# Two attention/SwiGLU layers in fp32: the second projection's chunk 2 is turned earlier, its load moves on the DMA queue, and one closing step changes form

## The chip, the core and the metric

The kernel runs on one core of one Trainium2 chip. The metric is the device time of one launch in microseconds (us). Before the change the median of three runs is 1949.36 us (1948.67 to 1949.93).

## The reference

Two identical layers on `x` of shape 1 x 2048 x 448, in fp32; the weights of the second layer are those of the first:

```python
def A(x, wq, wk, wv, wo):          # 16 heads of 28, one shared key and value head
    q = (x @ wq).reshape(B, S, 16, 28).transpose(0, 2, 1, 3)
    k, v = x @ wk, x @ wv
    p = softmax(einsum("bhqd,bkd->bhqk", q, k) * 28 ** -0.5)
    return einsum("bhqk,bkd->bhqd", p, v).transpose(0, 2, 1, 3).reshape(B, S, 448) @ wo
def B(x, w_gate, w_up, w_down):    # inner width 1792
    return (silu(x @ w_gate) * (x @ w_up)) @ w_down
x = x + A(layernorm(x)); x = x + B(layernorm(x))
x = x + A(layernorm(x)); x = x + B(layernorm(x))
```

## The kernel before

The 2048 rows are four chunks of 512 (`NC`), each of four tiles of 128 rows. `xres` holds the running `x` in SBUF. Every fp32 product is made of three passes over split operands: a high part (`xh`, `wh`) and a remainder (`xl`, `wl`).

The order of instructions on each engine is the order in which the Python code issues them (`manual_schedule`): nothing is reordered, and the engines wait for each other by semaphores alone. So the order is written out by hand, with three helpers. `self.soon` is a list of `[count, function]`: each `unit` lowers all counts by one and runs, in list order, those that fall below zero. `a.plan[n, 0]` and `a.plan[n, 1]` hold functions that `project` runs ahead of and behind its n-th tile. `self.pend` holds the down step of the unit before and the additions that follow it.

Each layer runs in three stages: the projection (16 tiles numbered by `self.seen`, 0 to 15, four for each chunk), the scores with softmax and P-V, and the feed-forward. The feed-forward goes through 14 column tiles `fc` of the inner width in seven groups of two, and in each group through the four chunks; one `unit` makes one `fc` of one chunk, and `down` multiplies its result by `w_down` into four PSUM banks `d[0..3]`, one for each tile of 128 rows. `down` works in two half steps. In each, pairs of matmuls lie side by side, one over rows 0 to 63 of the contraction and one over rows 64 to 127 (`side_by_side`, L332). Behind the first half step ScalarE reads one column of each bank (`between`, L339), and the second half waits for that. For the very last step of the second layer alone, `by_tile` (L888) makes 12 matmuls over all 128 rows instead, bank after bank.

The change lies where the first layer's feed-forward passes into the second layer's projection. There `hand_over(c)` is called for each chunk when its last group is done:

- `turn` makes the normalized chunk (`xn`, VectorE L230), transposes it in 32 x 32 blocks (L268, into a buffer named `xh`), and sends it to DRAM with four DMAs of SyncE's queue (`send`, L274, to `xt`).
- `load` fetches it back with the transpose completed, into two idle query buffers `qstack` (SyncE L954, L955, L957).
- `parts` splits that into `xh` on ScalarE (L292, L296) and `xl` on VectorE (L293, L302).

Chunk 3 is turned on TensorE instead (`ready`, L230, then transposes L248 ahead of tile 8). Its additions (`accumulate`) come behind the closing down step: banks 0 and 1 are added by VectorE (L901), banks 2 and 3 are copied by ScalarE to a `stage` buffer (L904) and added by GpSimd (L905).

Each projected tile is stored (`q`, L545 to L556): ScalarE copies it twice (L545, L546), SyncE stores it to `qd` (L547) and, for the tiles with keys, to `kt` (L550); for the tiles with values VectorE transposes a strip (L553, `vt`) and GpSimd copies it in four pieces (L556, `vsb`). After tile 2 the queue also fetches eight keys, `few` (L405), from which VectorE builds `kdiag` (L409), used by the `maxima` matmuls (L438) behind tile 6.

Of the kernel before, what the change touches and what calls it, by code (L numbers as in the profile page):

```python
# [23 lines left out]
NC = S // 512  # L24
NG = H // 4
NF = F // P
# [29 lines left out]
def forward(  # L56
# [31 lines left out]
    phase, banks, threes, live, turn = ExitStack(), [], [], set(), {}  # L88
# [114 lines left out]
    def xtile(pool, again=None):  # L203

        return (
            pool.tile([P, 4, 512], F32R, name="xh"),
            pool.tile([P, 3, 512], F32R, name="xl"),
            again,
        )

    def norm_steps(c, pool=pers, twice=True):

        got = {}
        cs = slice(4 * c, 4 * c + 4)

        def stat(t):
            nc.vector.bn_stats(stats[:, 4 * c + t, :], xres[:, 4 * c + t, :])
            nc.vector.bn_aggr(mv[:, 4 * c + t, :], stats[:, 4 * c + t, :])

        def scale():  # L220
            rstd = pers.tile([P, 4], F32, name="rstd", bufs=2)
            nc.gpsimd.tensor_scalar(rstd, mv[:, cs, 1], 1.0, EPS, ALU.mult, ALU.add)
            nc.gpsimd.tensor_tensor(rstd, rstd, halfn, ALU.pow)
            got["r"] = rstd

        def apply(t):
            if t == 0:
                got["x"] = pool.tile([P, 4, 512], F32, name="xn")
            o, i, r = got["x"][:, t, 0:D], xres[:, 4 * c + t, :], got["r"][:, t : t + 1]
            nc.vector.tensor_scalar(o, i, mv[:, 4 * c + t, 0:1], r, ALU.subtract, ALU.mult)  # L230
            if twice:
                nc.gpsimd.tensor_copy(got["x"][:, t, D:512], o[:, 384:D])

        fs = [lambda t=t: stat(t) for t in range(4)] + [scale]
        return fs + [lambda t=t: apply(t) for t in range(4)], got
# [30 lines left out]
    def turn_tile(got, tb, t):  # L266

        nc.vector.transpose(tb[:, :, 32 * t : 32 * t + 32], got["x"][:, t, 0:D].rearrange("p (b w) -> p b w", w=32))  # L268

    def send(tb, raw):  # L270

        to = raw.rearrange("(b d) (g n) -> g d b n", d=32, g=4)
        for g in range(4):
            nc.sync.dma_start(to[g], tb[32 * g : 32 * g + 32])  # L274
# [11 lines left out]
    def halved(tiles, r, ks, copy, sub):  # L286

        xh, xl, xd = tiles
        for k in ks:
            raw = r[k] if isinstance(r, list) else r[:, k, :]  # L290
            if k < 3:
                copy(xh[:, k, :], raw)  # L292
                sub(xl[:, k, :], raw, xh[:, k, :], ALU.subtract)  # L293
                continue
            if xd is None:
                copy(xh[:, 3, :], raw)  # L296
                high = xh[64:128, 3, :]
            else:
                copy(xd[64:128, :], raw[64:128, :])
                copy(xh[0:64, 3, :], raw[0:64, :])  # L300
                high = xd[64:128, :]
            sub(xh[64:128, 3, :], raw[64:128, :], high, ALU.subtract)  # L302
# [24 lines left out]
    def side_by_side(lower, upper):  # L327

        assert len(lower) == len(upper)
        for two in zip(lower, upper):  # L330
            for po, (a, b), start, stop in two:
                nc.tensor.matmul(po, a, b, start=start, stop=stop, skip_group_check=True)  # L332
# [3 lines left out]
    def between(*pos):  # L336

        for i, po in enumerate(pos):
            nc.scalar.copy(seen[:, i : i + 1], po[:, 0:1])  # L339
# [504 lines left out]
    groups = [range(f, min(f + FG, NF)) for f in range(0, NF, FG)]  # L844

    class FeedForward:
# [6 lines left out]
        def down(self, fs, fc, d, hh, hl):  # L853


            _, _, dh, dl = self.W[fc]
            if self.layer == 1 and d is self.dn.get(NC - 1) and fs is groups[-1]:
                return [lambda: self.by_tile(fs, fc, d, ((hh, dh), (hh, dl), (hl, dh))), lambda: None]
            self.flip = 1 - self.flip
            one, two = ((0, 1), (2, 3)) if self.flip else ((2, 3), (0, 1))  # L860

            def step(ts, first):
                lists = []
                for upper, half in enumerate(ts):
                    rs = slice(64 * upper, 64 * upper + 64)
                    lists.append(
                        [
                            (
                                d[t][:, 0:D],
                                (a[rs, P * t : P * t + P], b[rs, :]),  # L870
                                first and fc == fs[0] and z == 0,
                                not first and fc == fs[-1] and z == 2,
                            )
                            for t in half
                            for z, (a, b) in enumerate(((hh, dh), (hh, dl), (hl, dh)))
                        ]
                    )
                side_by_side(*lists)
                if first:
                    between(*d)  # L880

            return [lambda: step((one, two), True), lambda: step((two, one), False)]
# [36 lines left out]
        def hand_over(self, c):  # L919

            a = self.nxt
            fs, got = norm_steps(c, twice=c == NC - 1)
            for f in fs[:5]:
                f()
            a.pool = self.stage

            if c == NC - 1:

                def ready():
                    for f in fs[5:]:  # L930
                        f()
                    a.norms[c] = got

                a.X[c] = xtile(self.xbp)
                a.plan[5, 1] = [ready]
                return
            to = dram.tile([D, 512], F32, name=f"xt1_{c}")
            raw = [q.bitcast(F32)[:, z, :] for q in qts[1:] for z in range(2)]

            def turn():  # L940
                for f in fs[5:]:
                    f()
                pool = (xpool, self.x1p, self.xbp)
                tb = pool[min(c + 1, 2)].tile([P, 4, 512], F32R, name="xh").bitcast(F32)
                tb = tb.rearrange("p a (b n) -> p (a b) n", n=P)[:, 0 : D // 32, :]
                for t in range(4):
                    turn_tile(got, tb, t)
                send(tb, to)
                a.X[c] = xtile(pool[c])
                if c < 2:  # L950
                    load()

            def load():
                nc.sync.dma_start(qts[1].bitcast(F32), to[0:256, :].rearrange("(k p) n -> p k n", p=P))  # L954
                nc.sync.dma_start(raw[2], to[256:384, :])  # L955
                for half in (slice(0, 64), slice(64, 128)):
                    nc.sync.dma_start(raw[3][half, :], to[384:448, :])  # L957

            def parts():
                halved(a.X[c], raw, range(4), nc.scalar.copy, nc.vector.tensor_tensor)  # L960

            self.soon.append([1, turn])
            if c == 2:
                a.plan[4, 1] = [load]
                a.plan[7, 0] = [parts]
                return
            self.soon.append([3, parts])
            self.soon.append([4 - c, lambda: [a.project() for _ in range(2 - c)]])
# [160 lines left out]
    fs, got = norm_steps(0)  # L1129
# [23 lines left out]
    for c in range(1, NC):  # L1153
        fs, got = norm_steps(c)
# [39 lines left out]
```

## Time and profile before

| what | value |
|---|---|
| runs | 1949.36 us median, 1948.67 to 1949.93 |
| the profiled execution | 1949.26 us, its span 1947.5 us |
| TensorE busy | 1934.0 us, 99% of the span |
| ScalarE, VectorE, GpSimd busy | 1251.9, 980.8, 560.1 us |
| granted TensorE clock | 0.999 |
| first tile of the second projection | 969.1 us from the span's start |
| closing down step of the first layer | 987.1 to 990.6 us |
| first score matmul of the second layer | 1026.9 us |

The timeline gives for each instruction its start, its duration, its engine and line, and in square brackets how long the engine sat idle before it and what released it. Rows of equal neighbours are merged with a count, and the duration is then that of the whole row. Matmuls overlap in the pipeline, so the distance between two starts is what one costs. A row "SPq" is the issue of a DMA by SyncE; the transfer comes after it.

### The profile page before, as it was taken

The page shows a single profiled execution, that of the slowest core. Times are in us where ns is not written, and L with a number is a line of the kernel's source. Part 1 is how long each engine was busy: PE and PEld are TensorE (multiplying, and loading weights), DVE is VectorE, ACT ScalarE, POOL GpSimd, SP SyncE. Part 2 cuts the span into 40 slices and gives each one's busy share as a digit, 9 for nine tenths or more (in the row PEclk, how much of TensorE's full clock was granted, in tenths as well). Part 3 has the DMA queues.
Part 4 walks back from the last instruction along what each step waited for, and adds up shares of the span by engine and source line. Part 5 has one row for each costly group of instructions (what it writes and reads, how often), then busy time and mean ns, then how long its engine had stood idle before and what let it go on. Part 6 is the DMA issues. An engine that isn't in the chain of part 4 may idle for free. (4 is left out here: it accounts for less than half of the span.)

```text
span 1947.5 us, 43868 instructions
## 1 busy us (share of the span) xinstructions
PE 1934.0 (99%) x18393; PEld 1311.6 (67%) x18393; DVE 980.8 (50%) x1675; ACT 1251.9 (64%) x1871; POOL 560.1 (29%) x596
## 2 busy tenths in 40 slices
PE   9999999999999999999999999999999999999998
PEld 7544545445468999999974445454454688888887
DVE  6665575665754222322666555757657432232223
ACT  4899898998953333333359998989989333333332
POOL 4213123122215333433341221122231352333420
PEclk9999999999999999999999999999999999999999
DMA  5111011021122011100251110110221220011102
GB/s 166 57 35 30 22 40 41 23 58 31 32 81 73 17 32 32 33 22 22 63 157 43 34 34 21 40 39 24 57 50 31 77 62 25 17 32 32 33 1 77
DMA packets 105475, 87.54 MB, mean 45 GB/s; under 512 B 25304, under 2 KB 85464, under 8 KB 105272
## 3 DMA queue, kind: packets, MB, share of 16 engines
q1 hardware_dynamic: 103576, 83.25, 15.5%
q8 instruction: 145, 2.38, 0.5%
q10 hardware_dynamic: 1696, 1.43, 0.2%
q14 instruction: 58, 0.48, 0.1%
HBM read 59.48 MB, written 23.33 MB: 43 GB/s over the span
## 5 line engine op out<-in xcount | busy, mean ns | idle before, releaser
L662 ACT ACTIVATE pt<-three 128x1536 f32<-128x1536 f32 x512 | 731.2, 1515 | 52.7 <-PE three L640 52.7
L695 PE MATMUL bank<-pt,vsb 128*32 128x512 f32 x3072 | 490.8, 598 | 0.0
L695 PE MATMUL bank<-pair,vsb 128*32 128x512 f32 x1024 | 487.4, 598 | 0.6 <-ACT pair L663 0.6
L640 PE MATMUL bank<-qstack,keys 32*128 32x512 f32 x1536 | 471.8, 425 | 0.0
L640 PE MATMUL three<-qstack,keys 32*128 32x512 f32 x4608 | 428.7, 408 | 0.5 <-ACT stage L546 0.3
L640 PEld LDWEIGHTS bank<-qstack,keys 32*128 32x128 f32 x1536 | 243.3, 183 | 248.1 <-issue 124.6
L661 DVE COPY pair<-bank 128x512 f32<-128x512 f32 x512 | 354.3, 692 | 95.1 <-PE bank L640 60.0
L332 PE MATMUL bank<-xh,wgh 64*128 64x512 f32 x1712 | 357.4, 389 | 0.0
L1025 DVE TENSOR_TENSOR sg<-bank,sg 128x512 f32<-128x512 f32 x112 | 77.4, 691 | 485.4 <-ACT sg L1024 474.7
L332 PE MATMUL bank<-xh,wgl 64*128 64x512 f32 x1391 | 310.7, 390 | 0.0
L332 PE MATMUL bank<-wdh,h 64*128 64x448 f32 x1760 | 303.3, 363 | 1.0 <-DVE h L1031 0.6
L663 ACT ACTIVATE pair<-pair 128x1024 f32<-128x1024 f32 x256 | 289.6, 1131 | 0.0
L640 PEld LDWEIGHTS three<-qstack,keys 32*128 32x128 f32 x4608 | 261.8, 183 | 14.2 <-DVE xres L611 1.5
L332 PE MATMUL bank<-xl,wgh 64*128 64x512 f32 x1284 | 268.5, 389 | 0.0
L695 PEld LDWEIGHTS bank<-pt,vsb 128*32 128x32 f32 x3072 | 101.7, 109 | 246.2 <-issue 153.2
L905 POOL TENSOR_TENSOR xres<-stage,xres 128x448 f32<-128x448 f32 x107 | 126.7, 1204 | 480.5 <-ACT stage L904 480.2
L703 DVE TENSOR_TENSOR o<-bank,o 128x512 f32<-128x512 f32 x224 | 155.0, 692 | 202.3 <-PE bank L695 202.3
L339 ACT COPY seen<-bank 128x1 f32<-128x1 f32 x654 | 74.9, 164 | 253.3 <-PE bank L332 252.7
L1024 ACT ACTIVATE sg<-bank 128x512 f32<-128x512 f32 x112 | 67.2, 600 | 215.9 <-PE bank L332 210.8
L332 PEld LDWEIGHTS bank<-xh,wgh 64*128 64x128 f32 x1712 | 182.0, 184 | 18.4 <-issue 1.0
L332 PEld LDWEIGHTS bank<-wdh,h 64*128 64x128 f32 x1760 | 183.2, 184 | 15.5 <-issue 1.7
L332 PE MATMUL bank<-wdl,h 64*128 64x448 f32 x880 | 174.7, 367 | 0.0
(149 smaller groups left out, 2105.8 us busy)
## 6 DMA issues: line engine op xcount, KB each, us to landing
o<-rd SPq DMA_DIRECT2D x32, 256.0 KB
qraw<-qd SPq DMA_DIRECT2D x128, 56.0 KB
xt<-tb SPq DMA_DIRECT2D x32, 224.0 KB
wdr<-in_B_w_down_dram SPq DMA_DIRECT2D x28, 224.0 KB
xn<-xt SPq DMA_DIRECT2D x8, 768.0 KB
wr<-in_B_w_gate_dram SPq DMA_DIRECT2D x28, 192.0 KB
wr<-in_B_w_up_dram SPq DMA_DIRECT2D x28, 192.0 KB
qd<-stage SPq DMA_DIRECT2D x20, 224.0 KB
```

The source lines that it names most:

```text
L332: nc.tensor.matmul(po, a, b, start=start, stop=stop, skip_group_check=True)
L339: nc.scalar.copy(seen[:, i : i + 1], po[:, 0:1])
L640: nc.tensor.matmul(three[:, j, :] if j < 3 else one, k[js, kp, ks], q[js, part, :], start=(z == 0), stop=(z == 2), tile_position=(32 * j, 0),)
L661: copies.append(nc.vector.tensor_copy(pt1, one))
L662: es.append(nc.scalar.activation(pt, threes[y], AF.Exp, scale=SCALE))
L663: es.append(nc.scalar.activation(pair, pair, AF.Exp, scale=SCALE))
L695: nc.tensor.matmul(to[32 * j : 32 * j + 32, :], vsb[:, n % NT, :], pts[n][j], start=(y == 0), stop=(y == 1), skip_group_check=True,)
L703: f = nc.vector.tensor_tensor(accs[i][:, 0, :], to, accs[i][:, 0, :], ALU.add)
L905: nc.gpsimd.tensor_tensor(r, s, r, ALU.add)
L1024: nc.scalar.activation(in_order(sg, True), natural(pg[0], True), AF.Silu)
L1025: nc.vector.tensor_tensor(in_order(sg, True), natural(pg[1], True), in_order(sg, True), ALU.mult)
```

## The change

It makes three edits, all at the hand-over from the first layer's feed-forward to the second layer's projection.

```diff
@@ down
-            if self.layer == 1 and d is self.dn.get(NC - 1) and fs is groups[-1]:
+            if d is self.dn.get(NC - 1) and fs is groups[-1] and (self.layer == 1 or fc == NF - 1):
                 return [lambda: self.by_tile(fs, fc, d, ((hh, dh), (hh, dl), (hl, dh))), lambda: None]
@@ hand_over
-            self.soon.append([1, turn])
+            self.soon.insert(0 if c == 2 else len(self.soon), [1, turn])
             if c == 2:
-                a.plan[4, 1] = [load]
+                a.plan[4, 0] = [load]
                 a.plan[7, 0] = [parts]
                 return
```

First, on VectorE, behind the last `h` of the first layer's feed-forward (L1031): chunk 2's `turn` (L230, L268) and chunk 1's split (`xl`, `xh` from `qstack`) change places. `vt` is the value strip of tiles 2 and 3, `few` and `kdiag` belong to the maxima.

```order
 L1025 TENSOR_TENSOR sg<-bank_6453,sg 128x512
 L1031 TENSOR_TENSOR h_11444<-sg,h_11444 128x512
+L230 TENSOR_SCALAR xn<-xres,mv,rstd 128x448 x4
+L268 STREAM_TRANSPOSE xh<-xn 128x14x32 x4
 L293 TENSOR_TENSOR xl<-qstack_101,xh 128x512 x2
 L293 TENSOR_TENSOR xl<-qstack_102,xh 128x512
 L302 TENSOR_TENSOR xh<-qstack_102,xh 64x512
 L553 STREAM_TRANSPOSE vt<-bank_6454 32x512
-L230 TENSOR_SCALAR xn<-xres,mv,rstd 128x448 x4
-L268 STREAM_TRANSPOSE xh<-xn 128x14x32 x4
 L553 STREAM_TRANSPOSE vt<-bank_6451 32x512
 L409 TENSOR_TENSOR kdiag<-few,mask 112x512
```

The eight instructions of the turn move ahead of the split and of the first `vt`; from the second `vt` on the order is the old one.

Second, on SyncE's queue at the same place: the four sends of chunk 2 (L274) and the stores of tile 2, tile 3 (both `qd_0`) and tile 4 (`qd_1`, `kt_1`).

```order
+L274 DMA xt_2_11349<-xh 32x14x128 x4
 L547 DMA qd_0_11361<-stage 112x512
 L405 DMA few<-kt_0_789 112x1x8
-L274 DMA xt_2_11349<-xh 32x14x128 x4
 L547 DMA qd_0_11361<-stage 112x512
-L547 DMA qd_1_11593<-raw 112x512
-L550 DMA kt_1_790<-raw 12x512
 L954 DMA qstack_101<-xt_2_11349 128x2x512
 L955 DMA qstack_102<-xt_2_11349 128x512
 L957 DMA qstack_102<-xt_2_11349 64x512 x2
+L547 DMA qd_1_11581<-raw 112x512
+L550 DMA kt_1_790<-raw 12x512
```

The sends now stand ahead of tile 2's store and of `few`, and the load stands ahead of the two stores of tile 4.

Third, on TensorE, the closing down step of chunk 3 in the first layer: 24 matmuls over half the rows become 12 over all rows. The end of the old rows and the beginning of the new ones, with the four banks of `d`:

```order
-L332 MATMUL bank_78<-wdh,h_11444 128x448
-L332 MATMUL bank_6456<-wdh,h_11444 128x448
-L332 MATMUL bank_79<-wdh,h_11444 128x448
-L332 MATMUL bank_6456<-wdl,h_11444 128x448
-L332 MATMUL bank_79<-wdl,h_11444 128x448
-L332 MATMUL bank_6456<-wdh,h_11444 128x448
-L332 MATMUL bank_79<-wdh,h_11444 128x448
+L888 MATMUL bank_6455<-wdh,h_11444 128x448
+L888 MATMUL bank_6455<-wdl,h_11444 128x448
+L888 MATMUL bank_6455<-wdh,h_11444 128x448
+L888 MATMUL bank_6456<-wdh,h_11444 128x448
+L888 MATMUL bank_6456<-wdl,h_11444 128x448
```

The new rows fill bank after bank; on ScalarE the four one-column reads of `between` (L339) that stood inside this step are gone, so that the copies to `stage` (L904) follow the copies of tile 3 directly.

## The prediction

> **What bounds the kernel now.** I read the page first, then TensorE's waits, then the timeline of each engine between 960 and 1030 us.
>
> ```profile
> span 1947.5 us, 43868 instructions
> PE 1934.0 (99%) x18393; PEld 1311.6 (67%) x18393; DVE 980.8 (50%) x1675; ACT 1251.9 (64%) x1871; POOL 560.1 (29%) x596
> ```
>
> TensorE is the bound, with 13.5 us of its span idle. An edit of order can win only at TensorE's pauses and at steps that TensorE itself does slowly. Around the change there are two such places. The first is the closing down step of the first layer; the last two rows are the second layer's closing steps, already in full rows.
>
> ```profile
> 986.77 0.39 PE L312 MATMUL bank<-xh,wl 128*128 128x512 f32 x1
> 987.09 0.47 PE L332 MATMUL bank<-wdh,h 64*128 64x448 f32 x2
> ...
> 989.21 0.47 PE L332 MATMUL bank<-wdh,h 64*128 64x448 f32 x1 [0.36 <-ACT seen L339]
> ...
> 990.63 0.50 PE L312 MATMUL bank<-xh,wh 128*128 128x512 f32 x1
> ...
> 1936.92 0.37 PE L888 MATMUL bank<-wdh,h 128*128 128x448 f32 x1
> ...
> 1941.64 0.37 PE L888 MATMUL bank<-wdh,h 128*128 128x448 f32 x1
> ```
>
> The step lasts from 987.09 to 990.63, 3.54 us, with a wait for ScalarE's `seen` in its middle. The second place is the start of tile 8, the first tile of chunk 2:
>
> ```profile
> 1001.74 1.91 PE L248 MATMUL bank<-ident,xn 128*128 128x128 f32 x16
> 1004.13 0.50 PE L312 MATMUL bank<-xh,wh 128*128 128x512 f32 x1 [0.47 <-ACT xh L292]
> 1004.85 0.50 PE L312 MATMUL bank<-xl,wh 128*128 128x512 f32 x1 [0.22 <-DVE xl L293]
> ```
>
> The transposes of chunk 3 pass (L248); then tile 8 waits 0.47 us for `xh` of chunk 2 and 0.22 us for its `xl`. From 1004.85 to the score stage at 1026.87 us TensorE runs without a pause of that size, so whatever the second matmul of tile 8 gains or loses, the end gains or loses. That one start, **1004.85 us, is my measuring point**.
>
> **The closing step.** 24 matmuls L888 take 23 gaps from 1936.92 to 1941.64, 0.205 us each; 12 take 2.46 us. The pause at a change between the two forms goes too (986.77 to 987.09 is 0.32 us; between neighbours of one form it is 0.23), so the step starts at 987.0 and tile 4 at 989.46 instead of 990.63. That is 1.17 us won on TensorE, if tile 8 lets it through. Tiles 4 to 7 do: their inputs, the split of chunk 1, come from the row of VectorE, next. The four `seen` copies on ScalarE cost nothing beside that wait.
>
> **The turn ahead of the split, on VectorE.**
>
> ```profile
> 983.36 1.89 DVE L293 TENSOR_TENSOR xl<-qstack,xh 128x512 fp32r<-128x512 f32 x3
> ...
> 986.00 0.72 DVE L553 STREAM_TRANSPOSE vt<-bank 32x512 f32<-32x512 f32 x1
> 986.76 1.85 DVE L230 TENSOR_SCALAR xn<-xres,mv,rstd 128x448 f32<-128x448 f32 x4
> 988.53 2.21 DVE L268 STREAM_TRANSPOSE xh<-xn 128x448 f32<-128x448 f32 x4
> 990.77 0.72 DVE L553 STREAM_TRANSPOSE vt<-bank 32x512 f32<-32x512 f32 x1
> 991.53 0.69 DVE L409 TENSOR_TENSOR kdiag<-few,mask 112x512 fp32r<-112x512 f32 x1
> 992.25 1.16 DVE L901 TENSOR_TENSOR xres<-bank,xres 128x448 f32<-128x448 f32 x2
> ...
> 996.20 0.63 DVE L217 BATCH_NORM_STATS2 stats<-xres 128x6 f32<-128x448 f32 x1 [0.58 <-POOL xres L905]
> ...
> 998.46 1.78 DVE L230 TENSOR_SCALAR xn<-xres,mv,rstd 128x448 f32<-128x448 f32 x4 [1.42 <-POOL rstd L223]
> ...
> 1002.53 0.72 DVE L553 STREAM_TRANSPOSE vt<-bank 32x512 f32<-32x512 f32 x1
> 1004.11 1.94 DVE L293 TENSOR_TENSOR xl<-qstack,xh 128x512 fp32r<-128x512 f32 x3 [0.85 <-ACT xh L292]
> ```
>
> The turn takes 986.76 to 990.74, 3.98 us, and the split 983.36 to 986.00, 2.64 us. In the new order the turn ends at 983.36 + 3.98 = 987.34 instead of 990.74, 3.4 us earlier; the split runs from there to 989.98 and the first `vt` to 990.73, 4.0 us later. The second `vt` still stands at 990.76. The split stays covered: its first third is there at 988.0, and tile 4 reads it from 989.7 on at a third each 0.68 us, against 0.65 us for VectorE. Cover of some 1.6 us is left.
>
> **The load.** Sent 3.4 us earlier and no longer behind tile 4's stores, the load can be issued when the sends have landed.
>
> ```profile
> 969.97 3.01 SPq L274 DMA_DIRECT2D xt<-xh  x4
> 976.19 0.38 SPq L954 DMA_DIRECT2D qstack<-xt  x1
> ...
> 985.80 0.30 SPq L547 DMA_DIRECT2D qd<-stage  x1
> 986.21 0.69 SPq L405 DMA_DIRECT2D few<-kt  x1
> 990.77 3.01 SPq L274 DMA_DIRECT2D xt<-xh  x4
> 993.88 1.13 SPq L547 DMA_DIRECT2D qd<-stage  x1
> ...
> 998.34 0.39 SPq L954 DMA_DIRECT2D qstack<-xt  x1
> ```
>
> For chunk 1 the load followed the first send by 6.22 us. So it goes out at 987.34 + 6.22 = 993.6 instead of 998.34, and with 5.1 us to the first `xh` (998.34 to 1003.46 in ScalarE's row below) the data is there at 998.7. ScalarE's wait is gone, and the 0.47 us with it. But what is late next? VectorE reaches `xl` only when its own row lets it: in the old trace it was free for `xl` at 1003.25, behind the `vt` of 1002.53, and waited just 0.85 us. So the load alone could win at most 0.85 us, and only if VectorE's row up to there is not later. It is later, and this is the part that decides.
>
> **What the sends are moved past.** Tile 2's store and `few` now stand behind the four sends on SyncE's queue. Who waits for them?
>
> ```profile
> 990.16 0.53 ACT L904 COPY stage<-bank 128x448 f32<-128x448 f32 x1 [0.95 <-ACT seen L339]
> 994.37 0.53 ACT L904 COPY stage<-bank 128x448 f32<-128x448 f32 x1 [3.67 <-POOL xres L905]
> ...
> 1003.46 1.70 ACT L292 CAST xh<-qstack 128x512 fp32r<-128x512 f32 x3 [3.42 <-DMA qstack<-xt]
> ```
>
> ```profile
> 986.86 1.43 POOL L556 COPY vsb<-vt 32x64 f32<-32x64 f32 x4 [10.10 <-DVE vt L553]
> 991.56 1.53 POOL L556 COPY vsb<-vt 32x48 f32<-32x48 f32 x4 [3.27 <-DVE vt L553]
> 993.17 1.17 POOL L905 TENSOR_TENSOR xres<-stage,xres 128x448 f32<-128x448 f32 x1
> ```
>
> `kdiag` needs `few`, and behind `kdiag` stand on VectorE the additions, chunk 3's statistics, its `xn`, and at last `xl`. The first L904 writes the `stage` buffer that tile 2's store reads, so it needs that store's end; behind it follow the first L905 (993.17), the second L904, which takes the same buffer again, the second L905, and the last statistics (996.20, released by it). Both chains meet at chunk 3's `xn` (998.46); call its start X. From X to the second matmul of tile 8 it is 4.81 us to the end of `vt` (998.46 to 1003.25, and 0.02) and 0.74 us from the start of `xl` to that matmul (1004.11 to 1004.85): X + 5.55. The balance against 1004.85 is X = 999.3.
>
> *Tile 2's store.* It is issued at 990.45, behind 3.1 us of sends. The nearest row is tile 3's store at 993.88, also behind four sends: it took 1.13 us to issue (0.30 for the one at 985.80). Its data was not through before 997:
>
> ```profile
> 975.00:976.00 1.00, 1.00 (x12) 0.83 (x10) 0.34 (x2) 0.53 (x2) 0.46 (x2) 1.00 0.40 102
> ...
> 996.00:997.00 1.00, 1.00 (x6) 0.82 (x5) 0.77 (x2) 0.99 (x4) 0.16 (x1) 1.00 0.80 178
> 997.00:998.00 1.00, 1.00 (x6) 0.84 (x5) 0.04 (x1) 1.00 (x3) 0.79 (x2) 1.00 0.37 131
> ```
>
> The DMA share (the column before the last) is 0.80 up to 997 and 0.37 behind, so data ended near 997.4, 6.6 us behind the first send at 990.77. Here that is 987.34 + 6.6 = 993.95. Landing is later than the data's end: chunk 1's sends ended near 975.4 (share 0.40 in that microsecond) and the load that waits for them came at 976.19, 0.8 us on. So 994.7; the floor is the sends' own landing at 993.6. L904 0.6 us, then from L905 to X as before (993.17 to 998.46, 5.29): X = 1000.6, 1.3 us over the balance.
>
> *`few`.* Issued at 991.6 to 992.3. Floor again 993.6; ceiling: before, `kdiag` did not wait at 991.53, 4.63 us from the issue's end at 986.90, so 996.9. I take 994.8, just behind the store, nearer the floor as it is small. From `kdiag` to X: 0.72 (to L901), 1.07 (two additions), three statistics of 0.73, and 2.26 us from the last one's start to X (996.20 to 998.46): 6.24. X = 1001.0, and the measuring point is 1006.6, **1.7 us later than before**. The floor gives X = 999.8 and 0.5 us, the ceiling 3.8 us.
>
> [...]
>
> **The sum.** Closing step −1.17 and load −0.69 on TensorE, both swallowed by VectorE's later `xl`: net +1.7. The profiled execution took 1949.26 us (1.76 us more than its span, and 0.1 under the median): 1949.3 + 1.7 = **1951.0 us**. Its own range is 1949.8 to 1952.8.
>
> **The rivals.**
>
> 1. *The store and `few` land early* (small or short transfers don't queue behind the sends). Then GpSimd's row decides: the first `vt` ends at 990.73, its four `vsb` pieces at 992.3, the second four and their gap (991.56 to 993.17, 1.61 us) at 993.95, so L905 starts 0.8 us later than before, X = 999.25, the measuring point where it was: 1949.2 us, between 1948.1 and 1949.8. For it: `few` is small. Against: 0.8 DMA share for as long as the sends last.
> 2. *`kdiag` becomes TensorE's own wait.* The maxima matmuls (L438) come at 997.1 in the new order (989.46 and 33 matmuls, 7.66 us before). If `few` lands after 996.4, TensorE waits there as well, and each further microsecond is one at the end. If it lands after 997.0, the loss is over 3.9 us: 1953.2 and more, say 1954. Against it stands only the ceiling of 996.9, in a quieter queue.
> 3. *Both pauses vanish whole* (VectorE's chain does not depend on store or `few` as I read it): −1.17 and −0.7, 1947.4 us. It needs chunk 3's `xn` ahead of 998.5 with GpSimd 0.8 us later; I find no slack for that.
>
> **How the numbers follow.** 0.2%, 3.9 us, is about what a measurement of this kernel can tell from no change. Chances: forecast 0.60, rival 1 0.25, rival 2 0.10, rival 3 0.03; 0.02 stays for a gain over 3.9 us, more than all pauses here together. So within 0.2% has 0.60 + 0.25 + 0.03 = 0.88, slower 0.10, faster 0.02. The range takes the forecast's and most of rival 1: 1948.4 to 1952.8.
>
> **What would show it.** In the new profile: 12 rows L888 from 987.0, tile 4 at 989.5; the load's L954 near 993.6; a wait of VectorE ahead of `kdiag` for the DMA of `few`, 3 us long; the first L904 near 994.7 behind a DMA; chunk 3's `xn` at 1001; TensorE idle some 2 us ahead of L248 (the transposes need L440, 1.71 us after X, to have read their bank) and again ahead of tile 8's `xl`; first score matmul near 1028.6. I am wrong if `kdiag` starts before 993 (rival 1), if TensorE waits ahead of L438 (rival 2), or if the score stage behind 1027 us runs at another pace.

## The result, and the profile after

After the change the median is 1951.51 us (1950.52 to 1953.87, 22 runs) against 1949.20 us of before (1948.32 to 1950.11, 22 runs): ratio 1.0013, 95% interval 1.0007 to 1.0019. The change costs 2.3 us, 0.13%, which is measured as a loss and lies inside the 0.2% that the prediction took as its bound. The profiled execution took 1951.60 us, 2.34 more than the profiled execution of before.

The head of the page, and the first row of TensorE's waits (what waited for what, us in total, times, the longest):

```profile
span 1949.9 us, 43834 instructions
PE 1934.9 (99%) x18381; PEld 1332.8 (68%) x18381; DVE 977.1 (50%) x1675; ACT 1252.1 (64%) x1867; POOL 560.4 (29%) x596
```

```profile
PE bank L248 <- DVE sg L440: 3.2, 1, 3.2
```

TensorE's longest wait in the whole kernel now stands ahead of the transposes of chunk 3, a place where before there was none. It waits for `sg` (L440), with which VectorE reads the bank that these transposes write next. TensorE's timeline (start, duration of the row, and in brackets the idle time before it):

```profile
986.70 0.40 PE L312 MATMUL bank<-xh,wl 128*128 128x512 f32 x1
986.93 0.37 PE L888 MATMUL bank<-wdh,h 128*128 128x448 f32 x1
...
989.40 0.40 PE L312 MATMUL bank<-xh,wh 128*128 128x512 f32 x1
...
1003.66 3.60 PE L248 MATMUL bank<-ident,xn 128*128 128x128 f32 x16 [3.15 <-DVE sg L440]
1006.98 0.51 PE L312 MATMUL bank<-xh,wh 128*128 128x512 f32 x1
1007.33 0.39 PE L312 MATMUL bank<-xl,wh 128*128 128x512 f32 x1
...
1029.09 0.50 PE L640 MATMUL bank<-qstack,keys 32*128 32x512 f32 x1
```

The closing step is shorter as planned: tile 4 starts 2.47 us after the first L888. But TensorE then idles for 3.15 us, and the 16 transposes take 3.60 us where they took 1.91. The second matmul of tile 8, the measuring point, comes at 1007.33 instead of 1004.85, the first score matmul at 1029.09 instead of 1026.87.

VectorE, and the rows of SyncE's queue, ScalarE and GpSimd that feed it:

```profile
983.31 1.78 DVE L230 TENSOR_SCALAR xn<-xres,mv,rstd 128x448 f32<-128x448 f32 x4
985.01 2.22 DVE L268 STREAM_TRANSPOSE xh<-xn 128x448 f32<-128x448 f32 x4
...
994.79 0.69 DVE L409 TENSOR_TENSOR kdiag<-few,mask 112x512 fp32r<-112x512 f32 x1 [3.70 <-DMA few<-kt]
...
1001.20 1.78 DVE L230 TENSOR_SCALAR xn<-xres,mv,rstd 128x448 f32<-128x448 f32 x4 [1.42 <-POOL rstd L223]
1002.89 0.71 DVE L440 STREAM_TRANSPOSE sg<-bank 128x512 f32<-128x512 f32 x1
```

```profile
987.25 3.00 SPq L274 DMA_DIRECT2D xt<-xh  x4
990.35 1.13 SPq L547 DMA_DIRECT2D qd<-stage  x1
991.58 1.04 SPq L405 DMA_DIRECT2D few<-kt  x1
992.71 0.43 SPq L547 DMA_DIRECT2D qd<-stage  x1
994.67 0.38 SPq L954 DMA_DIRECT2D qstack<-xt  x1
```

```profile
995.24 0.54 ACT L904 COPY stage<-bank 128x448 f32<-128x448 f32 x1 [7.03 <-DMA qd<-stage]
```

Both waits of the forecast are there: VectorE stands 3.70 us ahead of `kdiag` for the DMA of `few`, and ScalarE 7.03 us ahead of the first copy of the additions (L904) for tile 2's store. Chunk 3's `xn`, the prediction's X, starts at 1001.20 instead of 998.46.

The granted clock (PEclk, the third column from the right) around the long idle time:

```profile
1002.00:1003.00 1.00, 0.00 (x0) 0.00 (x0) 1.00 (x4) 1.00 (x4) 1.00 (x3) 1.00 0.33 35
1003.00:1004.00 1.00, 0.34 (x2) 0.35 (x3) 0.96 (x2) 1.00 (x3) 0.28 (x2) 0.82 0.64 123
1004.00:1005.00 1.00, 1.00 (x7) 1.00 (x6) 0.90 (x4) 1.00 (x4) 0.00 (x0) 0.50 0.88 207
...
1006.00:1007.00 1.00, 1.00 (x8) 1.00 (x6) 0.99 (x2) 0.73 (x2) 0.85 (x2) 0.50 0.44 146
1007.00:1008.00 1.00, 1.00 (x6) 0.85 (x5) 0.98 (x2) 0.69 (x2) 0.96 (x2) 0.97 0.21 74
```

It was 1.00 while TensorE stood idle and 0.50 when the transposes ran. The 0.82 and the 0.97 of the two slices at the edges put the slow stretch at 1003.6 to 1007.1. At this place it is new against before, and it was in no part of the prediction.

### The profile page after: what moved, and what is told of

The parts are those of the page before. It is cut to its first block, busy times and chain, and to the rows that moved or that the text cites. A ratio compares the mean times of both kernels' runs of the same rounds, so it can differ in the third digit from the quotient of the medians.

```text
span 1949.9 us, 43834 instructions
## 1 busy us (share of the span) xinstructions
PE 1934.9 (99%) x18381; PEld 1332.8 (68%) x18381; DVE 977.1 (50%) x1675; ACT 1252.1 (64%) x1867; POOL 560.4 (29%) x596
## 5 line engine op out<-in xcount | busy, mean ns | idle before, releaser
L332 PE MATMUL bank<-xh,wgh 64*128 64x512 f32 x1712 | 371.3, 389 | 0.0
L332 PE MATMUL bank<-xh,wgl 64*128 64x512 f32 x1391 | 320.4, 390 | 0.0
L663 ACT ACTIVATE pair<-pair 128x1024 f32<-128x1024 f32 x256 | 283.3, 1107 | 0.0
L332 PE MATMUL bank<-xl,wgh 64*128 64x512 f32 x1284 | 278.8, 389 | 0.0
L905 POOL TENSOR_TENSOR xres<-stage,xres 128x448 f32<-128x448 f32 x107 | 126.8, 1205 | 483.4 <-ACT stage L904 483.2
L339 ACT COPY seen<-bank 128x1 f32<-128x1 f32 x650 | 74.8, 164 | 251.6 <-PE bank L332 250.8
L332 PEld LDWEIGHTS bank<-xh,wgh 64*128 64x128 f32 x1712 | 196.0, 184 | 13.3 <-issue 1.0
L332 PEld LDWEIGHTS bank<-wdh,h 64*128 64x128 f32 x1744 | 192.5, 184 | 11.1 <-issue 1.3
L332 PE MATMUL bank<-wdl,h 64*128 64x448 f32 x872 | 179.9, 367 | 0.0
```

What stands on the lines that cost most here:

```text
L663: es.append(nc.scalar.activation(pair, pair, AF.Exp, scale=SCALE))
L905: nc.gpsimd.tensor_tensor(r, s, r, ALU.add)
```

## The experiments

Three kinds of question were put: which edit makes the loss, which of the two displaced transfers makes it, and what the clock adds. The whole execution differs between runs by up to 3.3 us ahead of the change (the same matmul of tile 3 comes at 985.6 to 988.9 us), so I measure from a fixed point inside each trace: the start of tile 3's last matmul. From it come three distances in us: to X (chunk 3's `xn` on VectorE), to the second matmul of tile 8, and to the first score matmul.

| kernel | to X | to tile 8 | to the scores | median us | ratio to before |
|---|---|---|---|---|---|
| before | 11.69 | 18.08 | 40.10 | | |
| after | 14.50 | 20.63 | 42.39 | 1951.51 | 1.0013 [1.0007, 1.0019] |
| full rows alone | 11.73 | 18.18 | 40.19 | 1947.93 | 1.0001 [0.9992, 1.0010] |
| turn and load alone | 14.49 | 20.05 | 42.11 | 1950.24 | 1.0009 [1.0000, 1.0019] |
| sends behind store and `few` | 11.90 | 17.46 | 39.53 | 1947.75 | 0.9997 [0.9988, 1.0006] |
| TensorE kept busy | 14.43 | 20.00 | 42.04 | 1949.88 | 1.0010 [1.0001, 1.0019] |
| full rows and load | 11.68 | 17.25 | 39.32 | 1947.65 | 0.9998 [0.9989, 1.0007] |
| `few` alone ahead | 13.62 | 19.79 | 41.56 | 1952.16, one run | |
| store alone ahead | 13.31 | 18.88 | 40.96 | 1947.99, one run | |
| split first | | | 39.81 | 1948.47 | 1.0000 [0.9991, 1.0009] |
| transposes later | | | 38.09 | 1947.15 | 0.9992 [0.9983, 1.0001] |

Each median stands beside its own runs of before, whose medians were 1948.16 us for the first four experiments, 1948.51 for the next four and 1948.9 for the last. Most differences are too small for the medians, so the distances carry the argument and the ratios only have to agree. Each distance comes from one trace. Where kernels do not differ up to X it repeats within 0.1 us: 11.68 to 11.73 in three kernels that leave the order of the sends alone, 14.43 to 14.50 in three that move them.

**Full rows alone.** The edit of `down` alone; turn and load stay where they were.

> Only the closing down step in full rows; turn and load as before. My theory: chunk 3's xn starts where it did (998.5 us), the load lands where it did, so the 1.17 us won at the closing step turn into idle time ahead of tile 8, whose second matmul stays at 1004.85: 1949.2 us, same as before within 0.4 us. TensorE idle ahead of tile 8 grows from 0.7 to 1.9 us. Rival (the full rows pay by themselves): 1948.0 us.

```profile
1000.06 1.97 PE L248 MATMUL bank<-ident,xn 128*128 128x128 f32 x16 [0.39 <-DVE sg L440]
1003.32 0.50 PE L312 MATMUL bank<-xh,wh 128*128 128x512 f32 x1 [1.29 <-ACT xh L292]
1004.05 0.50 PE L312 MATMUL bank<-xl,wh 128*128 128x512 f32 x1 [0.23 <-DVE xl L293]
```

The 1.17 us that TensorE wins in the closing step come back as waits: 0.39 + 1.29 + 0.23 us, 1.9 in place of 0.7. The distance to tile 8 is 18.18, as before. The step's gain is real, and by itself worth nothing, because tile 8 waits for data whose time TensorE does not set.

**Turn and load alone.** The other two edits, with the closing step in its old form.

```diff
-            self.soon.append([1, turn])
+            self.soon.insert(0 if c == 2 else len(self.soon), [1, turn])
             if c == 2:
-                a.plan[4, 1] = [load]
+                a.plan[4, 0] = [load]
```

> The turn ahead of the split and the early load, with the closing step in half rows as before. My theory: the late part is VectorE's chain, not TensorE's: chunk 3's xn again near 1001.2, the second matmul of tile 8 at 1006.7, 1.9 us later than before: 1951.1 us. TensorE arrives at the transposes at 1001.7 and idles 1.9 us instead of 3.2; whether the granted clock drops after that is open: if it does, 0.6 us more, 1951.7. Rival (the full rows in the first layer cost the time): 1949.2 or less.

```profile
994.17 0.69 DVE L409 TENSOR_TENSOR kdiag<-few,mask 112x512 fp32r<-112x512 f32 x1 [3.65 <-DMA few<-kt]
1000.62 1.78 DVE L230 TENSOR_SCALAR xn<-xres,mv,rstd 128x448 f32<-128x448 f32 x4 [1.42 <-POOL rstd L223]
```

```profile
1003.08 1.96 PE L248 MATMUL bank<-ident,xn 128*128 128x128 f32 x16 [1.81 <-DVE sg L440]
1006.18 0.50 PE L312 MATMUL bank<-xl,wh 128*128 128x512 f32 x1 [0.91 <-DVE xl L293]
```

X is as late as in the changed kernel (14.49 and 14.50), so the loss comes from these edits alone. The idle time ahead of L248 is 1.81 us here, since TensorE arrives 1.2 us later, and the transposes keep their 1.96 us.

**Sends behind store and `few`.** On the changed kernel, the four sends are issued behind tile 2's store and `few`; VectorE keeps the new order.

```diff
-                send(tb, to)
+                a.at(2, lambda: send(tb, to)) if c == 2 else send(tb, to)
```

> All of the change, but chunk 2's four sends are issued behind tile 2's store and few; VectorE's order is that of the change. My theory (store and few, queued behind the sends, hold VectorE): kdiag waits no more, chunk 3's xn near 999.2, tile 8's second matmul near 1004.8: 1949.2 us, 2.3 under the change. Rival (the new order on VectorE and GpSimd is itself the cost, or the early load's traffic): xn at 1000.5 or later, 1951 us.

```profile
990.14 0.69 DVE L409 TENSOR_TENSOR kdiag<-few,mask 112x512 fp32r<-112x512 f32 x1
...
997.63 1.78 DVE L230 TENSOR_SCALAR xn<-xres,mv,rstd 128x448 f32<-128x448 f32 x4 [1.42 <-POOL rstd L223]
```

```profile
1000.09 1.97 PE L248 MATMUL bank<-ident,xn 128*128 128x128 f32 x16 [0.56 <-DVE sg L440]
1003.19 0.50 PE L312 MATMUL bank<-xl,wh 128*128 128x512 f32 x1 [0.91 <-DVE xl L293]
```

The wait ahead of `kdiag` is gone, X comes back from 14.50 to 11.90, tile 8 from 20.63 to 17.46. The place of the four sends on the queue holds the whole loss, and with the sends behind the change is 0.6 us better than before at both later points. X is 0.2 us behind before's: that is GpSimd, whose eight `vsb` pieces now end later, as rival 1 had it (0.8 us there). Its first L905 starts 6.61 us from the fixed point, 6.40 before.

**Which of the two: `few` or the store.** Two kernels put only one of them ahead of the sends. `few` alone ahead, in `turn`:

```diff
-                send(tb, to)
+                (a.when.pop(2, [lambda: None])[0]() if c == 2 else None); send(tb, to)
```

> All of the change, but few is fetched ahead of chunk 2's sends; tile 2's store stays behind them. My theory (few and the store hold two chains that meet at chunk 3's xn within 0.1 us of each other): kdiag no longer waits, but the first L904 still waits for the store's end, so the mark stays at 20.3 to 20.7. Rival (few alone): mark 18.1.

```profile
993.28 0.69 DVE L409 TENSOR_TENSOR kdiag<-few,mask 112x512 fp32r<-112x512 f32 x1
1002.48 1.78 DVE L230 TENSOR_SCALAR xn<-xres,mv,rstd 128x448 f32<-128x448 f32 x4 [1.42 <-POOL rstd L223]
```

```profile
997.23 1.08 ACT L904 COPY stage<-bank 128x448 f32<-128x448 f32 x2 [6.86 <-DMA qd<-stage]
```

The store alone ahead:

```diff
-                send(tb, to)
+                a.when.setdefault(2, []).insert(0, lambda: send(tb, to)) if c == 2 else send(tb, to)
```

> All of the change, but tile 2's store is issued ahead of chunk 2's sends; few stays behind them. My theory: the first L904 comes near the end of its matmuls, but kdiag still waits for few, so the mark stays at 20.0 to 20.7. Rival (the store alone): mark 18.1.

```profile
992.33 1.04 DVE L409 TENSOR_TENSOR kdiag<-few,mask 112x512 fp32r<-112x512 f32 x1 [2.37 <-DMA few<-kt]
998.91 1.78 DVE L230 TENSOR_SCALAR xn<-xres,mv,rstd 128x448 f32<-128x448 f32 x4 [1.42 <-POOL rstd L223]
```

I had expected either transfer alone to bring nearly the whole loss, 20.0 us or more to tile 8. Measured are 19.79 and 18.88. Against X with both ahead (11.90), the store behind the sends costs 1.72 us, `few` behind them 1.41 (0.35 of it because `kdiag` itself took 1.04 us in this trace instead of 0.69), both 2.60.

For `few` the reason is in the start of `kdiag`: it comes 8.09 us after tile 3's last matmul with both behind (994.79 less 986.70), and 6.73 with `few` alone behind (992.33 less 985.60). So the store ahead of `few` on the queue delays `few` by another 1.36 us; I had treated the two as independent. Most of that is the time to issue the store: counted from the same matmul, the issue of `few` begins at 4.88 us with the store ahead (991.58) and at 3.63 without (989.23), a difference of 1.25.

The store itself lands when it did: 7.8 us behind the first send with `few` out of its way (989.42 to 997.23), 8.0 with it behind (987.25 to 995.24). That it costs only 1.72 us has to do with a side effect of the first kernel: its second copy L904 runs right behind the first, where in all others it waits for GpSimd's L905. The way from the first copy to X is 0.71 us shorter by that (5.25 against 5.96 us). With the usual way X would stand at 14.33 instead of 13.62, and the store alone would cost 2.43 of the 2.60 us, nearly what I had expected. That is a sum over two traces; no kernel shows it.

**TensorE kept busy.** On the changed kernel, 24 transposes of a constant into an idle bank fill the pause ahead of L248.

```diff
-                flip(self.norms.pop(c), self.X[c])
+                _ = [nc.tensor.transpose(banks[(self.used + 1) % 4][:, 0:P], ident, ident) for _ in range(24 if self.layer else 0)]; flip(self.norms.pop(c), self.X[c])
```

> All of the change, with 24 transposes of the identity into a free bank on TensorE ahead of chunk 3's transposes; nothing reads them. Theory (the idle 3.15 us lower the granted clock to 0.50 for the 16 transposes that follow, and this makes the last 0.6 us and the wide spread of the runs): the clock stays 1.00, the transposes take 1.9 us instead of 3.6, tile 8's second matmul at 1006.75: 1950.9 us, spread under 1.2 us. Rival (the transposes are slow for another reason, such as their banks or ScalarE): 3.6 us again, 1951.5 us.

```profile
1000.37 2.78 PE L516 MATMUL bank<-ident 128*128 128x128 f32 x24
1003.61 1.97 PE L248 MATMUL bank<-ident,xn 128*128 128x128 f32 x16 [0.46 <-DVE sg L440]
...
1006.72 0.50 PE L312 MATMUL bank<-xl,wh 128*128 128x512 f32 x1 [0.91 <-DVE xl L293]
```

With no useful work more, tile 8 comes 0.63 us sooner (20.00 for 20.63) and the scores 0.35 us (42.04 for 42.39). The transposes take 1.97 us again. X comes 0.07 us sooner here, so the half clock costs 0.56 us at tile 8. The 0.91 us wait for `xl`, which it had covered in the changed kernel, is back. The other half of the expectation failed: the eleven runs spread by 2.05 us, not by less than 1.2, and those of full rows alone, whose trace has no such stretch, by 4.68. So this stretch is not shown to make the spread.

**Full rows and load.** The changed kernel without its turn: chunk 2 is turned where it was, behind chunk 1's split.

```diff
-            self.soon.insert(0 if c == 2 else len(self.soon), [1, turn])
+            self.soon.append([1, turn])
```

> Full rows and the early load, but the turn of chunk 2 stays behind the split, as before; so the sends stay behind tile 2's store and few, and only tile 4's two stores are passed. Mark: from the last matmul of tile 3 to the second of tile 8, 18.08 us before, 20.63 changed. My theory (VectorE's chain bounds tile 8, and it is not touched here): xn where it was, the load 1.3 us earlier, so xl starts as soon as VectorE is free, 0.85 us earlier: mark 17.2, 0.85 us less than before. Rival (the load in front of tile 4's stores costs): mark 18.1 or more.

```profile
1000.00 1.97 PE L248 MATMUL bank<-ident,xn 128*128 128x128 f32 x16 [0.34 <-DVE sg L440]
1003.10 0.50 PE L312 MATMUL bank<-xl,wh 128*128 128x512 f32 x1 [0.91 <-DVE xl L293]
```

This kernel differs from full rows alone by the load only. Moved past tile 4's stores, the load brings `xh` in time: the wait of 1.29 us ahead of tile 8 is gone, and tile 8 comes 0.83 us sooner than before (17.25 for 18.08). Turning chunk 2 earlier was not needed for that; the kernel that does so too, with its sends behind store and `few`, is even 0.2 us behind this one (17.46).

**Towards a better one.** What waits now is `xl` of chunk 2 and `sg`, both on VectorE. Starting from the kernel with the sends behind, the next one splits chunk 2 a tile earlier, makes chunk 3's `xn` behind tile 6 instead of 5, transposes it ahead of tile 11, and gives the maxima behind tile 6 a bank of their own. Of its edit, the lines beyond the sends:

```diff
-                a.plan[5, 1] = [ready]
+                a.plan[6, 1] = [ready]
...
-                a.plan[7, 0] = [parts]
+                a.plan[6, 0] = [parts]
...
-            if self.layer and self.seen == 8:
+            if self.layer and self.seen == 11:
...
-                self.maxima(self.seen // 4 - 1)()
+                self.maxima(self.seen // 4 - 1, banks[7] if self.layer and self.seen == 6 else None)()
```

> A version from the findings: sends behind tile 2's store and few; chunk 2's split ahead of tile 6, chunk 3's xn behind it, its transposes ahead of tile 11 instead of tile 8; tile 6's maxima in the last bank, so that tile 8's bank is free. My theory: TensorE has no wait left from the closing step to the scores, so that the 1.17 us and the two waits of 0.7 us are kept. Mark to the first score matmul (from the last matmul of tile 3: 40.10 before, 42.39 changed): 38.2, 1.9 us under before. Rival (another wait takes their place, at the transposes or at tile 12): 39.5 or more.

```profile
1013.99 0.50 PE L312 MATMUL bank<-xl,wh 128*128 128x512 f32 x1 [0.95 <-DVE xl L255]
...
1023.38 0.50 PE L312 MATMUL bank<-xh,wh 128*128 128x512 f32 x1 [0.81 <-DVE sg L440]
```

Tile 8 no longer waits, and two other pauses take its place: 0.95 us ahead of tile 12, since the transposes leave too little time for chunk 3's split, and 0.81 us ahead of tile 15, whose bank the maxima behind tile 14 still hold. The distance to the scores is 39.81, little better than before. The rival was right here. Both pauses have a cause that can be moved, which the last kernel does: `xn` back behind tile 5, the transposes ahead of tile 10, and a bank of their own for the last maxima. Against the kernel above (of the last line only the argument that changes):

```diff
-                a.plan[6, 1] = [ready]
+                a.plan[5, 1] = [ready]
...
-            if self.layer and self.seen == 11:
+            if self.layer and self.seen == 10:
...
-banks[7] if self.layer and self.seen == 6 else None
+banks[{6: 7, 14: 6}[self.seen]] if self.layer and self.seen in (6, 14) else None
```

> As b1 (sends behind store and few, split of chunk 2 a tile earlier, full rows), but chunk 3's xn stays where it is in the changed kernel (beside tile 5) and only chunk 3's transposes are moved, ahead of tile 10 instead of tile 8; the maxima of the third group of tiles get a bank of their own, so the last of them no longer waits for sg. Mark: start of tile 3's last matmul to the first score matmul (before 40.10 us, after 42.39, b1 39.81). My theory (the pauses of b1 ahead of tiles 12 and 15 came from the later xn and from the shared bank): both pauses go, no idle ahead of tile 8, mark 38.2 to 38.7 us, 1.4 to 1.9 us less than before, median 0.1% under before's. Rival (VectorE's row is simply full here, and whatever is moved ahead makes something else late): another pause of 0.8 us or more between tile 8 and the first score, mark at or over 39.4, median within 0.03% of before's.

```profile
986.93 0.40 PE L312 MATMUL bank<-xh,wl 128*128 128x512 f32 x1
...
1001.25 0.50 PE L312 MATMUL bank<-xl,wh 128*128 128x512 f32 x1 [0.28 <-DVE xl L293]
...
1025.02 0.50 PE L640 MATMUL bank<-qstack,keys 32*128 32x512 f32 x1
```

One wait of 0.28 us is left between tile 3 and the scores. The distance is 38.09 us, 2.0 less than before and 4.3 less than after. The median is 1947.15 us against 1948.9, ratio 0.9992, interval 0.9983 to 1.0001. In the trace it beats both kernels at this place. Each against its own runs of before, it also beats the changed kernel, whose interval (1.0007 to 1.0019) lies above; against before its interval just reaches no change.

## Why the prediction was right, and where its terms were off

1951.0 us was forecast; the profiled execution took 1951.6 and the median is 1951.51. The mechanism was right: the sends hold up the store and `few`, these hold up chunk 3's `xn`, and that holds up tile 8. Which of the two chains ends last it had the wrong way round, and one term was missing. The measurement also tells this loss of 0.13% from no change, which the prediction, with its 0.2%, did not expect. By its steps:

- **The closing step.** 12 rows L888 from 986.93, tile 4 at 989.40, forecast 987.0 and 989.46. Shown by the first experiment: 1.17 us, all swallowed at tile 8.
- **The load.** Forecast near 993.6; it was issued at 994.67, 7.42 us behind the first send instead of the 6.22 taken from chunk 1. In the other kernels that load the same way this distance is 6.30 (store alone ahead) to 7.39 us (turn and load alone). What makes the difference was not tested. It did not count: `xl` came later than `xh` in any case.
- **`few` and `kdiag`.** Forecast 994.8 for its landing, measured 994.79. So close a hit is luck: 994.8 was picked between a floor of 993.6 and a ceiling of 996.9. From `kdiag` to X 6.24 us were forecast, which would give 1001.03; X came at 1001.20.
- **The store.** The first L904 came at 995.24, forecast 994.7, half a microsecond later than thought. From it to X it is 5.96 us, so this chain, not that of `few`, ends last in the profiled execution, by 0.17 us:

```profile
997.74 1.16 POOL L905 TENSOR_TENSOR xres<-stage,xres 128x448 f32<-128x448 f32 x1 [0.64 <-ACT stage L904]
```

```profile
998.06 0.59 DVE L217 BATCH_NORM_STATS2 stats<-xres 128x6 f32<-128x448 f32 x1
998.69 0.18 DVE L218 BATCH_NORM_AGGREGATE mv<-stats 128x2 f32<-128x6 f32 x1
998.93 0.63 DVE L217 BATCH_NORM_STATS2 stats<-xres 128x6 f32<-128x448 f32 x1
```

The second L905 ends at 998.90, and the last statistics (L217) start at 998.93, 0.24 us behind the start of the row ahead of them, where the two before started 0.10 us behind theirs. In the kernel with TensorE kept busy `few` decides instead: L904 comes at 994.81, `kdiag` at 994.92, and from there to X it is 6.23 us. The prediction put the two chains 0.4 us apart, with `few` behind; that they end so close together is why X was hit all the same. That both together are the cause, the kernel with the sends behind shows.

- **From X to tile 8.** Forecast X + 5.55. At full clock it is so: 5.56 us with turn and load alone, 5.57 with TensorE kept busy. In the changed kernel it was 6.13, because the transposes ran at half clock. This 0.58 us is the term that was missing.
- **The idle time ahead of L248.** Forecast "some 2 us", measured 3.15. The forecast lets the transposes start 1.71 us after X, where L440 starts (1001.20 and 1002.89). They need its end, another 0.71 us on: L440 ends at 1003.60, L248 starts at 1003.66. The wait for `xl` behind it, which was forecast too, did not come: the slow transposes hid it.
- **The sum.** 1.7 us forecast at tile 8; with 0.27 us more to X (14.50 from the fixed point, 14.23 forecast) and 0.58 for the clock it comes to 2.55, which is what the distances give (20.63 less 18.08). Of that 0.25 us are given back inside tile 8: from its second matmul to the first of tile 9 it is 2.52 us after the change (1007.33 to 1009.85) and 2.77 before (1004.85 to 1007.62). From there on both kernels run alike: 2.29 us at the first score, 2.34 at the end.

Rival 1 falls with the 3.70 us wait ahead of `kdiag`, rival 2 because TensorE never waited ahead of the maxima (L438 at 996.90, `kdiag` done at 995.48), rival 3 with X.

What the runs show is that a transfer issued behind the sends lands late: moved ahead of the sends, `few` and the store cause no wait at all; `few` alone behind the sends lands 6.2 us after the first of them (986.13 to 992.33), with the store in between 7.5 (987.25 to 994.79). They do not show that it waits inside the DMA engines. In the changed kernel SyncE stands 7.0 us ahead of the sends until the turn is done and then takes 3.0 us to issue them, and the store and `few` stand behind in its row. `few` lands 2.2 us after the end of its issue (992.62 to 994.79), 2.0 us with the store ahead (990.31 to 992.33). Its lateness could be that of its issue alone. For the store there is more: it lands 3.8 us after its issue ended (991.48 to 995.24), and within 3.0 where the sends are behind it (985.07 to 988.05).

The forecast's floor of 993.6, which lets the store and `few` land no sooner than the sends, is shown by no run. In its place they show `few` landing within 0.12 us of the load's issue, which waits for the sends: 994.79 and 994.67 after the change, 992.33 and 992.43 with the store alone ahead; the store itself landed at 995.24. Whether either could have landed sooner was not tested.

## What to carry to other kernels

When a step is moved ahead, list what its DMAs overtake on their queue, and follow each displaced transfer to the instruction that waits for it. Here a transfer of 3.5 KB behind sends of 4 x 224 KB landed 6.2 us after the first of them, and the store between them delayed it by another 1.36. Moving the consumer on VectorE cost 0.2 us at X and moving the sends was the whole loss, so the two belong in separate edits. A gain on the busiest engine counts only as far as the next wait for data: the closing step's 1.17 us were worth nothing alone, step and load together brought 0.8 us, and two only came once VectorE's row and the banks behind it were rearranged as well.

## What was not expected of the hardware

The pause of TensorE cost more than its length where the clock fell: 0.56 us more at tile 8 of the changed kernel, against the kernel that is kept busy there. After 3.15 us of idle time (the changed kernel) the 16 transposes ran at a granted clock of 0.50 and took 3.60 us; the same happened after 2.28 us:

```profile
1004.95 3.61 PE L248 MATMUL bank<-ident,xn 128*128 128x128 f32 x16 [2.28 <-DVE sg L440]
```

This is the kernel with `few` alone ahead. After 1.97 us (the store alone ahead) and 1.81 us (turn and load alone) they took 1.97 and 1.96 us. A second place fits: ahead of the kernel's very first transposes TensorE stands idle too, and how long differs from run to run. In before's trace it was 2.32 us, and the clock fell there as well (in the second view PEclk is the third column from the right):

```profile
9.35 3.84 PE L248 MATMUL bank<-ident,xn 128*128 128x128 f32 x16 [2.32 <-DVE xn L230]
```

```profile
11.00:12.00 1.00, 1.00 (x8) 1.00 (x7) 0.00 (x0) 1.00 (x4) 0.55 (x1) 0.57 1.05 389
```

In the changed kernel's trace that pause was 1.04 us, and the clock stayed at 1.00 (8 to 17 us).

The low clock lasted 3.4 us each time: from 1003.6 to 1007.1 in the changed kernel, from 1005.1 to 1008.5 with `few` alone ahead, from 11.1 to 14.5 in before's trace. In the first two it began within 0.2 us of the pause's end; in before's trace 1.8 us after the pause ahead of L248 had ended, so the length of the pause does not settle it alone. Whether between 1.97 and 2.28 us lies a limit, or something else decided, these traces don't tell.

The 22 runs of the changed kernel spread by 3.35 us, those of before by 1.8. The eight with a mean granted clock of 0.998 or less have a median of 1952.65 us, the other fourteen 1951.17. One slow stretch of 3.4 us is 0.0009 of the mean clock, so these eight must have had more low clock than this one stretch. The kernel's start is one place where it can lie; where it lay in these eight, the runs without a trace don't show.

A store's issue behind the four sends took 1.13 us of SyncE's queue, 0.30 us in the quiet queue of before; that of `few` took 1.04 us, 0.69 before.
